# A one-core transformer block in float32: the first modulation rows, the first high parts and the first three projections rearranged

## The chip, the core and the metric

The kernel runs on one core of a Trainium2 chip. The time is the device time of one execution in microseconds (us). Before the change three timed runs took 1871.35, 1871.86 and 1875.66 us, median 1871.86 us. One more execution was taken with the hardware profiler: it took 1873.81 us, of which 1872.1 us are the span from its first to its last instruction.

## What is computed

The reference, cut to what matters here (x is 2048 x 576, c is 1 x 576, w_mod is 576 x 3456):

```python
mod = (silu(c) @ w_mod).reshape(1, 6, 1, 576)
sa, ca, ga, sb, cb, gb = ...            # six modulation vectors of 576
h = layernorm(x) * (1 + ca) + sa
x = x + ga * A(h)                       # q, k, v projections; attention with memory in 4 segments of 512 rows; wo
h = layernorm(x) * (1 + cb) + sb
x = x + gb * B(h)                       # SwiGLU with 4608 hidden columns
```

Only the first line for `sa` (shift) and `ca` (scale), the first `h`, and the projections to q and k lie in the part that changes. The rest follows it.

## The kernel before, in words

Matrix products are made to nearly float32 accuracy from two parts: an operand is cast to fp32r (the high part, `hi`), the remainder is the low part, and a product is high x high + low x high + high x low. `split` (L84) does this with a POOL cast (L85) and a DVE subtraction (L86).

**Head (0 to about 45 us).** SP starts the loads in the order of the program: `cs` (the vector c) and `gat` (beta), then six tiles `wm` of w_mod, each with two row groups of 96 rows and one of the two slices (L336), between them the four row tiles of x of segment 0, in numbers given by `XP`, then the weights `wraw` of the q and k projection (L297), four of them before a buffer must come free. TensorE multiplies silu(c), copied into 32 columns (`sgb`), by `wm` (L362): for each slice and each of six row groups two matmuls, columns 0:256 and 256:576, into two 32-partition groups of the PSUM tile `pr`. These write rows; a row is copied to SBUF by ACT (L366, L369), turned into columns by three transposes (`pcr`, L373), and DVE puts scale (+1) and shift into `colv` (L376 to L378).

The rows of x are normalized by DVE and POOL, and transposed by TensorE in five blocks `pt` of 128 columns (L240, two PSUM buffers). `evac_split` (L242) takes each block: ACT applies scale and shift (`hf`, L247), POOL casts the high part `hh` (L85), DVE subtracts to the low part `hl` (L86); the fifth block has 64 columns, and its high and low parts share the tile `hr`. The weights go through `split` on POOL and DVE too (`wqkh`, `wqkl`).

**Projections.** `proj` (L462) makes one 128 x 512 block `pp` of q or k from 14 matmuls (L105, `mm14`): three for each of four blocks and two with `hr`. There are nine per segment and three PSUM buffers for them, which the value projection `pv` shares. ACT copies `pp` to `pf` (L470), `split` makes `fh` (POOL) and `fl` (DVE), and SP writes them to DRAM (`kD`, `qD`, `qF`). `phi_k` transposes the k blocks (`ptk`, L441). `pf`, `fh` and `fl` have two buffers each. The four segments s = 0 to 3 run this way until about 245 us; from segment 1 on the first attention steps, which need DVE, are laid between the matmuls.

**What sets the order.** The program is recorded in the order of the code; a scheduler then places each engine's instructions by readiness and priority. Within an engine the instructions run in that order, TensorE's matmuls too. SP starts the DMAs in its own order, and an instruction that waits there holds up the ones behind it.

Of the kernel before, what the change touches and what calls it, by code (L numbers as in the profile page):

```python
# [11 lines left out]
ALU = mybir.AluOpType  # L12
# [38 lines left out]
HP = (0, 1, 2)  # L51
XP = (3, 1, 0, 0, 0, 0)
LD = 2
# [24 lines left out]
@with_exitstack  # L78
def block(ctx: ExitStack, tc: tile.TileContext, x, wqk, wv, wo, beta, wgu, wgr, wd, c, w_mod, out):
    nc = tc.nc  # L80
# [161 lines left out]
    def evac_split(wk, pt, kt, hi, lo, sc, bi, tag="hf"):  # L242
        f = wk.tile([P, L], F32, tag=tag, name="hf")
        n = P if kt < 4 else 64
        if kt == 4:
            hi, lo = hi[0:64], hi[64:128]
        nc.scalar.activation(f[:n], pt[:n], AF.Identity, scale=sc[:n], bias=bi[:n])  # L247
        split(hi, lo, f[:n])

    with ExitStack() as p1:  # L250
# [28 lines left out]
        cs = wk.tile([96, 6], F32, tag="cs", name="cs")  # L279
        nc.sync.dma_start(cs, c)  # L280
        nc.sync.dma_start(gat, beta.partition_broadcast(P))
        xs = {}
# [46 lines left out]
        with ExitStack() as p0:  # L329
            m0 = pool(p0, "m0")  # L330
            wm = {}
            gx = load_x(0)
            for p in (1, 0):
                for k in range(3):
                    wm[p, k] = m0.tile([96, 2, D], F32, tag=f"wm{p}{k}", name=f"wm{p}{k}")
                    nc.sync.dma_start(wm[p, k], wmv[p][:, 2 * k:2 * k + 2, :])  # L336
                    for _ in range(XP[3 * (1 - p) + k]):
                        next(gx)

# [16 lines left out]
            pr = ps.tile([P, L], F32, tag="m", name="pr", bufs=1)  # L356
            for p in (1, 0):
                for k in range(6):
                    for h in range(2):
                        r = 64 * (1 - p) + 32 * h  # L360
                        w = wm[p, k // 2][:, k % 2, 256:576] if h else wm[p, k // 2][:, k % 2, 0:256]
                        nc.tensor.matmul(pr[r:r + 32, :320 if h else 256], lhsT=sgb[:, k, :], rhs=w,  # L362
                                         start=(k == 0), stop=(k == 5))
            row = wk.tile([P, L], F32, tag="hf", name="row")[:, :320]
            nc.gpsimd.memset(row[:, 256:], 0.0)
            nc.scalar.copy(row[:, :256], pr[:, :256])  # L366
            for p in (1, 0):
                r = 64 * (1 - p) + 32
                nc.scalar.copy(row[r:r + 32, 256:], pr[r:r + 32, 256:320])  # L369
            pc = ps.tile([P, 3, P], F32, tag="m", name="pcr", bufs=1)  # L370
            for b in range(3):
                n = P if b < 2 else 64
                nc.tensor.transpose(pc[:n, b, :], row[:, 128 * b:128 * b + n], ident)  # L373
            for p in (1, 0):
                c0 = 64 * (1 - p)
                nc.vector.tensor_scalar(colv[:, 0:2, 1 - p], pc[:, 0:2, c0], float(p), None, op0=ALU.add)  # L376
                nc.vector.tensor_scalar(colv[:, 2:4, 1 - p], pc[:, 0:2, c0 + 32], float(p), None, op0=ALU.add)
                nc.vector.tensor_scalar(colv[0:64, 4:5, 1 - p], pc[0:64, 2, c0 + 32:c0 + 33], float(p), None, op0=ALU.add)  # L378

# [68 lines left out]
        def mem(s):  # L448
            for t in range(5):
# [10 lines left out]
                yield  # L460

        def proj(s, t):  # L462
            hh, hl, hr = hT[s]
            pp = ps.tile([P, L], F32, tag="p", name="pp", bufs=3)
            mm14(pp, lambda k: wqkh[:, t, k, :], lambda k: wqkl[:, t, k, :], lambda k: hh[k],
                 lambda k: hl[k], lambda: hr, True)
# [3 lines left out]
            nc.scalar.copy(f, pp)  # L470
            split(fh, fl, f)
            k0, k1 = 128 * t, min(128 * t + 128, D)
            if k0 < D:
                n = k1 - k0
                nc.sync.dma_start(kD[s][k0:k1, 0:2, :], f32(fh[:n]).unsqueeze(1).to_broadcast([n, 2, L]))
                nc.sync.dma_start(kD[s][k0:k1, 2, :], f32(fl[:n]))
            q0, q1 = max(128 * t - D, 0), 128 * t + 128 - D
            if q1 > 0:
                n = q1 - q0
                r = P - n  # L480
                nc.sync.dma_start(qD[s][q0:q1, 0:3:2, :], f32(fh[r:]).unsqueeze(1).to_broadcast([n, 2, L]))
                nc.sync.dma_start(qD[s][q0:q1, 1, :], f32(fl[r:]))
                if s > 0:
                    nc.sync.dma_start(qF[s][q0:q1, :], f[r:])
            return f
# [19 lines left out]

        for t in range(4):
            load_qk(t)
        for t in range(3):
            split_qk(t)
        for _ in trans_in(0):  # L510
            pass

        def load_wv():
            for k in range(5):
# [3 lines left out]
                yield  # L518

        for s in range(NSEG):  # L520
            gens = []
# [1171 lines left out]
```

## Time and profile before

| | |
|---|---|
| profiled execution | 1873.81 us |
| its span | 1872.1 us |
| median of three timed runs | 1871.86 us |
| busy TensorE (PE) | 1829.1 us, 98% of the span |
| busy VectorE (DVE) | 1492.9 us, 80% |
| busy ScalarE (ACT) | 1075.6 us, 57% |
| busy GpSimd (POOL) | 681.3 us, 36% |

The rows quoted below are of five kinds. A row of the timeline has the start, the time busy, the engine, the line, the operation with the tile that it writes and the tiles that it reads, and in brackets how long the engine was idle before it and who ended that. A row of the windows has the stretch, its length, the busy time of each engine with its instructions (x), the granted clock of TensorE, the share of the DMA engines and the GB/s. A group row has count, busy time and mean duration in ns. The slices of the page divide the span by 40. A matmul's end is modelled and runs past the next one's start, so I read the spacing of matmuls by their starts.

### The profile page before, as it was taken

What the parts mean: (1) busy time and instruction counts of PE and PEld (TensorE: products, weight loads), DVE (VectorE), ACT (ScalarE), POOL (GpSimd) and SP (SyncE); (2) the same over time, 40 slices, a digit from 0 to 9 for tenths busy, and PEclk for the clock granted to TensorE, in tenths of its full rate; (3) what the DMA queues carried; (4) which work ended last, traced back from release to release, by engine and by line L of the source; (5) the groups of instructions that cost most, each with busy time, mean ns of one, the idle gap of its engine ahead of it and who ended that gap; (6) DMA issues with size and microseconds to landing.
All of it is one profiled execution on the core that took longest, in us unless ns stands there. A gap on an engine that the chain in (4) does not pass through costs nothing.

```text
span 1872.1 us, 31670 instructions
## 1 busy us (share of the span) xinstructions
PE 1829.1 (98%) x10735; PEld 1546.2 (83%) x10735; DVE 1492.9 (80%) x3364; ACT 1075.6 (57%) x2330; POOL 681.3 (36%) x1173
## 2 busy tenths in 40 slices
PE   6999999999999999999999999989999999999999
PEld 4888876677776788888888888878888888888888
DVE  6565448788886699888888988857888888888886
ACT  1222258878877557777777777634454454544442
POOL 6212248776556657566565665400000000000000
PEclk9999999999999999999999999999999999999999
DMA  6766777677864954544545544485233332433331
GB/s 192 252 224 210 245 234 194 175 210 198 212 163 126 297 190 158 175 152 153 186 147 160 168 115 164 138 277 190 87 116 104 126 103 79 125 104 118 109 96 57
DMA packets 149912, 305.56 MB, mean 163 GB/s; under 512 B 30040, under 2 KB 60888, under 8 KB 147832
## 3 DMA queue, kind: packets, MB, share of 16 engines
q1 hardware_dynamic: 139144, 259.21, 46.2%
q10 hardware_dynamic: 10608, 44.34, 6.0%
q8 instruction: 85, 1.39, 0.3%
q14 instruction: 75, 0.61, 0.1%
HBM read 193.28 MB, written 109.64 MB: 162 GB/s over the span
## 4 chain that ended last, share of the span: by engine, by line
PE 86%; DVE 4%; DMA 4%; ACT 3%; issue 2%; POOL 1%; SPq 0%; POOLq 0%; ACTq 0%; DVEq 0%
PE A L1234 24%; PE pd L1353 19%; PE C L1234 12%; PE B L1234 6%; PE pp L105 5%; PE s L188 3%; PE av L627 3%; PE s L603 3%; PE pd L1373 2%; PE pw L737 2%; PE pv L105 2%; ACT Pt L610 1%; DMA y<-yD 1%; DVE junk L193 1%; PE pn L808 1%
## 5 line engine op out<-in xcount | busy, mean ns | idle before, releaser
L1234 PE MATMUL A<-y,wh 128*128 128x512 f32 x1152 | 405.4, 393 | 2.0 <-DMA y<-yD 1.3
L1361 DVE TENSOR_TENSOR acc<-acc,pd 128x576 f32<-128x576 f32 x327 | 245.3, 751 | 79.9 <-PE pd L1353 73.8
L193 DVE CUSTOM_DVE_ANT_0 junk<-s,tri 128x256 bf16<-128x256 f32 (+3 forms) x512 | 222.2, 484 | 66.2 <-PE s L188 49.1
L1353 PE MATMUL pd<-dh,ah 128*128 128x288 f32 x896 | 268.3, 299 | 1.1 <-DVE acc L1359 0.7
L1353 PE MATMUL pd<-dl,ah 128*128 128x288 f32 x896 | 264.2, 295 | 0.0
L1353 PE MATMUL pd<-dh,al 128*128 128x288 f32 x896 | 262.9, 293 | 0.0
L1234 PEld LDWEIGHTS A<-y,wh 128*128 128x128 f32 x1152 | 216.9, 188 | 41.1 <-issue 1.3
L1196 DVE TENSOR_TENSOR wl<-O,wh 128x256 fp32r<-128x256 f32 x504 | 239.5, 479 | 4.2 <-ACT wh L1195 3.5
L1234 PE MATMUL A<-y,wl 128*128 128x512 f32 x576 | 225.2, 391 | 0.0
L610 ACT ACTIVATE Pt<-s 128x512 f32<-128x512 f32 (+1 forms) x352 | 188.3, 559 | 43.2 <-PE s L603 21.1
L1234 PE MATMUL C<-y,wh 128*128 128x512 f32 x576 | 204.4, 396 | 3.0 <-DMA y<-yD 3.0
L1195 ACT CAST wh<-O 128x256 fp32r<-128x256 f32 x504 | 198.4, 406 | 1.9 <-POOL O L1189 1.6
L1353 PEld LDWEIGHTS pd<-dh,ah 128*128 128x128 f32 x896 | 168.4, 188 | 21.1 <-ACT pd L1329 4.0
L1299 DVE TENSOR_TENSOR al<-sg,ah 128x512 fp32r<-128x512 f32 x240 | 177.0, 738 | 8.5 <-ACT ah L1298 8.4
L1353 PEld LDWEIGHTS pd<-dl,ah 128*128 128x128 f32 x896 | 169.8, 189 | 16.0
L1189 POOL TENSOR_TENSOR O<-O 128x128 f32<-128x128 f32 x280 | 155.0, 586 | 69.2 <-DVE wl L1196 19.7
L1353 PEld LDWEIGHTS pd<-dh,al 128*128 128x128 f32 x896 | 169.4, 189 | 0.0
L1298 ACT CAST ah<-sg 128x512 fp32r<-128x512 f32 x240 | 149.1, 621 | 25.1 <-DVE sg L1258 24.1
L603 PE MATMUL s<-qs,ks 110*128 110x512 f32 (+2 forms) x384 | 149.0, 403 | 6.5 <-ACT Pt L610 4.7
L188 PE MATMUL s<-ks,qs 108*128 108x256 f32 (+3 forms) x512 | 142.4, 330 | 2.3 <-DVE mx L193 1.9
L1234 PEld LDWEIGHTS C<-y,wh 128*128 128x128 f32 x576 | 108.9, 189 | 22.5 <-DMA y<-yD 3.2
L1234 PEld LDWEIGHTS A<-y,wl 128*128 128x128 f32 x576 | 108.6, 188 | 14.8
(367 smaller groups left out, 4120.4 us busy)
## 6 DMA issues: line engine op xcount, KB each, us to landing
wr<-rD SPq DMA_DIRECT2D x216, 112.0 KB
O<-in_wgu_dram SPq DMA_DIRECT2D x36, 512.0 KB
oD<-O ACTq DMA_DIRECT2D x36, 512.0 KB
O<-oD SPq DMA_DIRECT2D x36, 512.0 KB
O<-in_wgu_dram SPq DMA_DIRECT2D x36, 384.0 KB
ks<-kD SPq DMA_DIRECT2D x32, 384.0 KB
qs<-qD SPq DMA_DIRECT2D x64, 192.0 KB
y<-yD SPq DMA_DIRECT2D x11, 1024.0 KB
```

The lines of the kernel that those rows point to most:

```text
L188: nc.tensor.matmul(bank[:, n * (h - h0):n * (h - h0) + n], lhsT=qst[b][0:108, h, 128 * i:128 * i + 128], rhs=kst[b][0:108, h // 2, 0:n], s ...
L193: nc.vector.tensor_tensor_reduce(junk[:, :n], bank[:, n * (h - h0):n * (h - h0) + n], tri[:, L - n:], 1.0, -3e38, op0=ALU.add, op1=ALU.max ...
L603: nc.tensor.matmul(bank[:, n * (g - h):n * (g - h + w)].rearrange("p (a b) -> p a b", a=w), lhsT=kst[u % NB][0:110, g // 2, 128 * j:128 * ...
L610: nc.scalar.activation(pt[:, h:h + per, :n], bank[:, :n * per].rearrange("p (a b) -> p a b", a=per), AF.Exp, scale=SCALE)
L1189: eng.tensor_tensor(o[:, d, i, s_], o[:, a, i, s_], o[:, b, i, s_], op=op)
L1195: nc.scalar.copy(wh, o)
L1196: later.append(lambda: nc.vector.tensor_tensor(wl, o, f32(wh), op=ALU.subtract))
L1234: nc.tensor.matmul(bank, lhsT=a, rhs=b, start=(first and n == 0), stop=(n == 6), skip_group_check=not first)
L1298: nc.scalar.copy(ah, src)
L1299: later.append(lambda: nc.vector.tensor_tensor(al, src, f32(ah), op=ALU.subtract))
L1353: nc.tensor.matmul(pd[:, i, :288], lhsT=a[:, tk], rhs=w, start=(add and k == 0), stop=(k == 2), skip_group_check=not add)
L1361: nc.vector.tensor_tensor(o, o, pd[:, :, :288], op=ALU.add)
```

## The change

Six edits.

1. w_mod is given a second time as `w_mod0`: for each of the six row groups k, 96 partitions with slices 1 (scale) and 0 (shift) side by side, 4608 contiguous bytes per partition. One DMA loads both slices of a row group (six DMAs, as before, of the same size).
2. For each row group four matmuls are issued, one for each of four 32-partition groups of `pr`: two slices x two column ranges (0:320 and 256:576), all 320 columns wide. There are 24, as before. One ACTIVATE takes all rows out and adds 1 to the scale rows through the bias `half`; three DVE copies fill `colv` in place of six additions.
3. `cs` and `gat` are loaded from ACT's queue. Two x tiles go ahead of the first `wm`, by `XP = (2, 1, 1, 0, 0, 0)`. The load of the first `wraw` stands in the code just behind `wm`.
4. In `evac_split`, in all four segments, ACT writes the high part straight out of PSUM (L250), then `hf` (L251); POOL has no part in it.
5. In `proj`, in all segments, ACT casts `fh` straight out of PSUM (L481), DVE subtracts it from PSUM into `fl` (L482), and ACT copies `pf` last (L484), and not at all for segment 0 from block 5 on.
6. The first three projections of segment 0 are written interleaved, block by block (`proj3`, L468).

```diff
-XP = (3, 1, 0, 0, 0, 0)
+XP = (2, 1, 1, 0, 0, 0)
...
+    half = cst.tile([P, 1], F32, tag="half", name="half")
+    nc.gpsimd.memset(half[0:64], 1.0)
+    nc.gpsimd.memset(half[64:128], 0.0)
...
+        nc.scalar.activation(hi, pt[:n], AF.Identity, scale=sc[:n], bias=bi[:n])
         nc.scalar.activation(f[:n], pt[:n], AF.Identity, scale=sc[:n], bias=bi[:n])
-        split(hi, lo, f[:n])
+        nc.vector.tensor_tensor(lo, f[:n], f32(hi), op=ALU.subtract)
...
-        nc.sync.dma_start(cs, c)
-        nc.sync.dma_start(gat, beta.partition_broadcast(P))
+        nc.scalar.dma_start(cs, c)
+        nc.scalar.dma_start(gat, beta.partition_broadcast(P))
...
-            for p in (1, 0):
-                for k in range(3):
-                    wm[p, k] = m0.tile([96, 2, D], F32, tag=f"wm{p}{k}", name=f"wm{p}{k}")
-                    nc.sync.dma_start(wm[p, k], wmv[p][:, 2 * k:2 * k + 2, :])
-                    for _ in range(XP[3 * (1 - p) + k]):
-                        next(gx)
+            for k in range(6):
+                wm[k] = m0.tile([96, 2, D], F32, tag=f"wm{k}", name=f"wm{k}")
+                for _ in range(XP[k]):
+                    next(gx)
+                nc.sync.dma_start(wm[k], w_mod0[k])
+            load_qk(0)
...
-            for p in (1, 0):
-                for k in range(6):
-                    for h in range(2):
-                        r = 64 * (1 - p) + 32 * h
-                        w = wm[p, k // 2][:, k % 2, 256:576] if h else wm[p, k // 2][:, k % 2, 0:256]
-                        nc.tensor.matmul(pr[r:r + 32, :320 if h else 256], lhsT=sgb[:, k, :], rhs=w,
-                                         start=(k == 0), stop=(k == 5))
+            for k in range(6):
+                for g in range(4):
+                    c0 = 256 * (g % 2)
+                    nc.tensor.matmul(pr[32 * g:32 * g + 32, :320], lhsT=sgb[:, k, :], rhs=wm[k][:, g // 2, c0:c0 + 320],
+                                     start=(k == 0), stop=(k == 5))
...
-            nc.gpsimd.memset(row[:, 256:], 0.0)
-            nc.scalar.copy(row[:, :256], pr[:, :256])
-            for p in (1, 0):
-                r = 64 * (1 - p) + 32
-                nc.scalar.copy(row[r:r + 32, 256:], pr[r:r + 32, 256:320])
+            nc.scalar.activation(row, pr[:, :320], AF.Identity, bias=half)
...
-                nc.vector.tensor_scalar(colv[:, 0:2, 1 - p], pc[:, 0:2, c0], float(p), None, op0=ALU.add)
...
+            for h in range(2):
+                nc.vector.tensor_copy(colv[:, 2 * h:2 * h + 2, :], pv[:, 0:2, :, h, 0])
+            nc.vector.tensor_copy(colv[0:64, 4, :], pv[0:64, 2, :, 1, 0])
...
+        def proj3():
+            hh, hl, hr = hT[0]
+            for t in QKORD[:3]:
+                first[t] = ps.tile([P, L], F32, tag="p", name="pp", bufs=3)
+            for kt, t in [(kt, t) for kt in range(3) for t in QKORD[:3]] + [(kt, t) for t in QKORD[:3] for kt in (3, 4)]:
+                h, l = wqkh[:, t, kt, :], wqkl[:, t, kt, :]
+                for a, b in ((h, hh[kt]), (l, hh[kt]), (h, hl[kt])) if kt < 4 else ((h, hr), (l, hr)):
+                    nc.tensor.matmul(first[t], lhsT=a, rhs=b, start=(kt == 0 and a is h and b is hh[0]),
+                                     stop=(kt == 4 and a is l))
...
-            nc.scalar.copy(f, pp)
-            split(fh, fl, f)
+            nc.scalar.copy(fh, pp)
+            nc.vector.tensor_tensor(fl, pp, f32(fh), op=ALU.subtract)
+            if s > 0 or t < 5:
+                nc.scalar.copy(f, pp)
...
+        proj3()
```

How the order moves, at three places. First TensorE at its start: the modulation matmuls `pr` (`wm` is w_mod, `sgb` the copied silu(c)), and the transposes `pt` of x. Before:

```order
L362 MATMUL pr<-wm_248,sgb 32x320
L240 MATMUL pt<-ident,x_244 128x128 x4
L362 MATMUL pr<-wm_251,sgb 32x256
L362 MATMUL pr<-wm_251,sgb 32x320
L362 MATMUL pr<-wm_251,sgb 32x256
L362 MATMUL pr<-wm_251,sgb 32x320
L240 MATMUL pt<-ident,x_244 128x128 x4
L362 MATMUL pr<-wm_253,sgb 32x256
```

Now, from TensorE's first instruction to the transposes of the row:

```order
L364 MATMUL pr<-wm_245,sgb 32x320 x4
L364 MATMUL pr<-wm_250,sgb 32x320 x4
L243 MATMUL pt<-ident,x_246 128x128 x2
L364 MATMUL pr<-wm_253,sgb 32x320 x4
L243 MATMUL pt<-ident,x_246 128x128 x3
L364 MATMUL pr<-wm_256,sgb 32x320 x4
L243 MATMUL pt<-ident,x_246 128x128 x3
L364 MATMUL pr<-wm_258,sgb 32x320 x4
L364 MATMUL pr<-wm_260,sgb 32x320 x4
L371 MATMUL pcr<-ident,row 128x128 x2
```

Each `wm` tile now feeds four matmuls of four partition groups in a row, and the eight transposes are spread over three places instead of two.

Second, TensorE behind the transposes of the row, where segment 0's projections begin. Before, it took the first matmul of the projection, two groups of transposes, and then what the scheduler saw as ready from two projections:

```order
L240 MATMUL pt<-ident,x_244 128x128 x4
L105 MATMUL pp<-hh_365,wqkh 128x512
L240 MATMUL pt<-ident,x_244 128x128 x4
L105 MATMUL pp<-hh_365,wqkl 128x512
L105 MATMUL pp<-hh_365,wqkh 128x512
L105 MATMUL pp<-hl_369,wqkh 128x512
L105 MATMUL pp<-hh_366,wqkh 128x512
L105 MATMUL pp<-hh_366,wqkl 128x512
L240 MATMUL pt<-ident,x_244 64x128 x4
```

Now:

```order
L468 MATMUL pp<-hh_360,wqkh 128x512
L468 MATMUL pp<-hh_360,wqkl 128x512
L468 MATMUL pp<-hh_360,wqkh 128x512
L243 MATMUL pt<-ident,x_246 128x128 x4
L468 MATMUL pp<-hh_360,wqkl 128x512
L468 MATMUL pp<-hh_360,wqkh 128x512
L468 MATMUL pp<-hh_360,wqkl 128x512
L468 MATMUL pp<-hl_364,wqkh 128x512
L243 MATMUL pt<-ident,x_246 128x128 x4
L468 MATMUL pp<-hl_364,wqkh 128x512 x2
L468 MATMUL pp<-hh_361,wqkh 128x512
L468 MATMUL pp<-hh_361,wqkl 128x512
```

Behind the second group of transposes stand four matmuls, then the last group of transposes, then 31 matmuls without a break. The two matmuls with `hr` of the first projection come behind 30 others; before they came behind 21.

Third, DVE between the normalization of x and the tile `hr`. Before:

```order
L376 TENSOR_SCALAR colv<-pcr 128x2
L377 TENSOR_SCALAR colv<-pcr 128x2
L378 TENSOR_SCALAR colv<-pcr 64x1
L86 TENSOR_TENSOR wqkl<-wraw,wqkh 128x640 x2
L86 TENSOR_TENSOR hl_369<-hf,hh_365 128x512
```

Now:

```order
L86 TENSOR_TENSOR wqkl<-wraw,wqkh 128x640
L374 COPY colv<-pcr 128x4 x2
L375 COPY colv<-pcr 64x2
L86 TENSOR_TENSOR wqkl<-wraw,wqkh 128x640 x2
L252 TENSOR_TENSOR hl_364<-hf,hh_360 128x512
L86 TENSOR_TENSOR wqkl<-wraw,wqkh 128x640
```

The first `wqkl` now stands ahead of `colv`. Outside segments 0 to 3 (from about 245 us on) no engine's order changes.

More of the change, by code (lines that the diff above doesn't have):

```diff
@@ L504, in vproj @@
                 nc.scalar.dma_start(vD[s], vs[s])
-        for t in range(4):
+        for t in range(1, 4):
             load_qk(t)
[L508 to L511, printed above, removed]
+        split_qk(0)
+        split_qk(1)
+        for kt, _ in enumerate(trans_in(0)):
+            if kt == 0:
+                split_qk(2)
         def load_wv():
```

17 lines of the change are left out of this document (9 added, 8 removed).

## The prediction

> **What bounds the kernel now.** I read the page first, then windows of the first 270 us, then the timeline of the first 50 us.
>
> ```profile
> span 1872.1 us, 31670 instructions
> ...
> PE   6999999999999999999999999989999999999999
> ```
>
> TensorE is full in every slice but the first (0 to 47 us): only there can the change win much. For segments 1 to 3, which it touches too, one window:
>
> ```profile
> 80.00:240.00 160.00, 158.34 (x917) 135.82 (x916) 87.71 (x207) 39.24 (x73) 40.20 (x64) 1.00 0.68 229
> ```
>
> TensorE idles 160.00 - 158.34 = 1.7 us there, and no edit can win more than that in this stretch, whatever it takes off POOL. So the sum is one of the head, up to the first matmul of the fourth projection; from there both kernels run the same matmuls.
>
> The head in the timeline, from the modulation rows to the ramp:
>
> ```profile
> 6.97 2.35 PE L362 MATMUL pr<-wm,sgb 96*32 96x256 f32 x8 [6.97 <-DMA wm<-in_w_mod_dram]
> ...
> 16.69 1.12 PE L240 MATMUL pt<-ident,x 128*128 128x128 f32 x4
> ...
> 17.74 5.32 PE L362 MATMUL pr<-wm,sgb 96*32 96x256 f32 x24
> ...
> 19.57 1.54 POOL L85 TENSOR_SCALAR wqkh<-wraw 128x640 fp32r<-128x640 f32 x2 [2.43 <-DMA wraw<-in_wqk_dram]
> ...
> 23.10 0.37 ACT L366 COPY row<-pr 128x256 f32<-128x256 f32 x1 [18.30 <-PE pr L362]
> ...
> 23.96 0.55 PE L373 MATMUL pcr<-ident,row 128*128 128x128 f32 x3 [0.89 <-ACT row L369]
> ...
> 24.93 1.45 ACT L247 ACTIVATE hf<-pt,colv 128x512 f32<-128x512 f32 x2 [1.03 <-DVE colv L376]
> ...
> 25.76 0.66 PE L240 MATMUL pt<-ident,x 128*128 128x128 f32 x4 [1.25 <-ACT hf L247]
> ```
>
> POOL reads the first `wraw` at 19.57 us. That is loaded behind the last `wm`, so `wm` is there before 19, but TensorE is busy with the rows until 17.74 + 5.32 = 23.06 us: they end late because TensorE is slow on them.
>
> Then the ramp, to the fourth projection:
>
> ```profile
> 36.42 1.03 DVE L86 TENSOR_TENSOR hr<-hf,hr 64x512 fp32r<-64x512 f32 x1
> ...
> 37.51 0.50 PE L105 MATMUL pp<-hr,wqkh 128*128 128x512 f32 x1 [2.00 <-DVE hr L86]
> ...
> 40.97 0.63 PE L105 MATMUL pp<-hh,wqkl 128*128 128x512 f32 x1
> 41.40 0.63 PE L105 MATMUL pp<-hl,wqkh 128*128 128x512 f32 x1
> ...
> 42.42 0.40 PE L105 MATMUL pp<-hl,wqkh 128*128 128x512 f32 x1
> 42.66 0.39 PE L105 MATMUL pp<-hh,wqkh 128*128 128x512 f32 x1
> ...
> 44.51 0.60 PE L441 MATMUL ptk<-ident,pf 128*128 128x128 f32 x4
> 44.87 0.48 PE L105 MATMUL pp<-hh,wqkh 128*128 128x512 f32 x1
> ```
>
> TensorE waits 2.0 us for `hr`, which DVE ends at 37.45 us, 12.5 us behind `colv`. At 44.87 us the fourth projection begins; 42 matmuls and two groups of `ptk` are done. Matmuls of 512 columns start 0.43 us apart at 41 us and 0.24 us apart at 42.5 us: the clock.
>
> **The clock** decides this change. First the durations of the row matmuls (lowest, median, highest, in ns), at their begin and at their end:
>
> ```profile
> L362 PE MATMUL pr<-wm,sgb x8: 604/688/742, 7.0 to 8.6; 96*32 96x256 f32 x4, 96*32 96x320 f32 x4
> ```
>
> ```profile
> L362 PE MATMUL pr<-wm,sgb x8: 380/432/507, 21.5 to 22.6; 96*32 96x320 f32 x5, 96*32 96x256 f32 x3
> ```
>
> The last ones take 0.63 of the first ones' time. The transposes at 16.69 us take 1.12 us for four, at 25.76 us 0.66 us. So the clock is half until about 21.6 us, though its column reads 1.00 there (it has no record before). It changes between windows of 3.41 us:
>
> ```profile
> 11.38:14.80 3.42, 3.42 (x14) 1.56 (x12) 1.97 (x6) 0.00 (x0) 3.42 (x6) 1.00 1.04 257
> ...
> 18.21:21.62 3.41, 3.41 (x18) 2.18 (x16) 0.00 (x0) 0.00 (x0) 1.45 (x2) 1.00 0.90 334
> ...
> 35.28:38.69 3.41, 1.41 (x6) 1.00 (x6) 3.35 (x4) 0.41 (x1) 1.64 (x2) 1.00 0.33 89
> 38.69:42.10 3.41, 3.41 (x12) 2.72 (x11) 2.90 (x5) 1.31 (x3) 2.75 (x4) 0.50 0.59 205
> 42.10:45.52 3.42, 3.42 (x18) 2.80 (x18) 3.36 (x5) 0.67 (x2) 1.14 (x2) 1.00 0.93 352
> ...
> 1260.66:1264.08 3.42, 2.55 (x10) 2.46 (x11) 0.00 (x0) 0.94 (x3) 0.00 (x0) 0.50 0.33 118
> ```
>
> A window with 1.41 us of work (35.28) is followed by one at half clock, and one full of matmuls (18.21, 38.69) by full clock. One with 2.55 us (1260.66) was still followed by half. The window from 11.38 us is full, yet the clock did not rise; of its work this much was transposes:
>
> ```profile
> 11.38:14.80 3.42, 1.12 (x4) 0.72 (x4) 1.00 1.04 257
> ```
>
> So 2.3 us of matmuls and 1.1 us of transposes do not raise the clock, and 3.41 us of matmuls do. I take it that transposes count little.
>
> **The change, step by step**, against the profiled execution (1873.81 us).
>
> *Loads.* Two SP issues leave the front, and the rates of the DMA engines from 10 to 20 us, in slices of 0.25 us, show what follows `wm`:
>
> ```profile
> 0.80 0.40 SPq L280 DMA_DIRECT2D cs<-in_c_dram  x1
> ...
> 1.72 0.43 SPq L336 DMA_DIRECT2D wm<-in_w_mod_dram  x1
> ```
>
> ```profile
> GB/s 267 277 323 415 249 212 276 286 240 230 267 295 267 212 277 277 184 286 277 286 267 221 258 258 258 258 276 267 300 193 267 230 277 317 379 420 379 389 410 389
> ```
>
> The first load is issued 0.92 us earlier. The rate is about 260 while `wm` flows and 390 from 18.3 us, for `wraw`: the last `wm` lands at about 18.7 us (estimate: 0.8 us before the first read of `wraw`, whose 328 kB take 0.8 us at 390). With the same bytes it would land at 17.8. Longer rows may help: no gain is one end, and the rate of `wraw` for all six tiles (2.65 MB: 10.2 us at 260, 6.8 at 390) the other, 14.4. I take 17, near the row of `wm` itself.
>
> The Trainium skill ("SBUF — State Buffer", Door 1: The DMA port swizzle) says that partitions 0 to 63 reach only half of the 16 DMA ports. Two thirds of a 96-partition tile share that half, so by it longer rows win nothing and the forecast moves 0.9 us up; if row length were the limit, TensorE would bound the rows at 17.1 and it moves 1.1 us down. No row of before tells these apart.
>
> *Rows.* Each of these matmuls shows as two records, so eight are two row groups of one slice. Their durations sum to 8 x 0.688 = 5.5 us but fit in 2.35 us: the two partition groups run beside each other, 1.1 us for each pair of row groups' matmuls at half clock, the time of the 320-column one alone. Before there are twelve such pairs. Four partition groups at once cost between 1.1 us (all beside each other) and 2.2 us (two and two) per row group. I take 1.1, since the two do not slow each other. The last `wm` at 17.0 and 1.1 us plus 0.2 us of tail give 18.3; TensorE's own work from the third tile on (4 x 1.1 + 6 x 0.28 us of transposes from about 12 us) gives 18.1. So the rows end at 18.2 instead of 23.06 us (bounds 17.1 and 19.1).
>
> *Row to column.* From 23.06 to 24.93 us it took 1.87 us. One ACTIVATE takes the place of three copies (-0.3 us), the three transposes run at half clock (+0.3), and the first `colv` copy costs as before. The `wqkl` now ahead of `colv` on DVE waits for a `wraw` that lands by 17.8, POOL's 0.77 us (two in 1.54 at 19.57) and about as long on DVE: 19.4, before the columns come at 20.0. If `wm` came a us later, both would move. ACT begins `hh` at 20.1 us.
>
> *Ramp.* `hh` takes about 0.75 us as `hf` does (two in 1.45 at 24.93), so TensorE starts at 20.9. Its clock is half: since the rows take half as long and the transposes lie between them, no window before is full of matmuls. It runs 11 matmuls (0.43) and three groups of transposes (1.1): 8.0 us, to 28.9. No window with such a group raises the clock, as at 11.38 us; the first window free of them begins 0 to 3.4 us behind 28.5 and ends 3.41 us later, at 33.6 on average (31.9 to 35.3). By then 11 more matmuls are done; the other 20 take 0.235 us each. The 42nd ends at 38.3 us (37.5 to 39.1). `ptk` of two blocks adds 0.9 and the wait for `pf` 0.1: 39.3 us against 44.87. **The head wins 5.6 us.**
>
> *What must be on time for that.* `hr` on DVE: with the same 12.5 us behind `colv` as before it comes at 32.6; five of some 12 POOL operations between them are gone, and TensorE needs it only behind 30 matmuls, at about 35.5. So the low parts and POOL's casts are hidden by the slow clock. Were the clock full, they would set the end.
>
> *Segments 1 to 3.* ACT gets five more ACTIVATEs of 0.75 us and nine casts of 0.59 us per segment, 9 us of some 60, beside the 25% that it is busy. POOL loses as many. Their price is 0, with -1.7 us (the idle time above) as one end; the other is the third rival.
>
> The sum: 1873.8 - 5.6 = 1868.2 us. The profiled execution lies 1.95 us above the median of the timed runs, so on their scale **1866.3**, and I say 1866.5.
>
> **Rivals.**
>
> *The clock rises early.* If transposes count as work, the first full window behind 20.9 ends at 26.0 on average. By then 7 matmuls and two groups are done; 35 matmuls and one group (0.66) take 8.9 us: 34.9 instead of 38.3, 3.4 us less: 1863. The window at 11.38 us speaks against it, but rows of 32 columns were the matmuls in it.
> The Trainium skill ("TensorE: Matmul & The Clock Gate", Part 4: PE-mode transpose) says that a transpose does not count as busy in the same way. By that rule the sum is mine; without it, this rival's. It speaks against thinning out the rows.
>
> *Only two partition groups run at a time.* Then the rows end at 22 to 23 us, `colv` comes at 24.5, the clock is full as before, and `hr`, 12.5 us later, sets the end: 37.0 + 12 x 0.235 + 1.0 = 40.8, a win of 4 us: 1868.
>
> *The third ends slower: the PSUM buffer of a projection is held longer.* It was free after ACT's copy; now the cast, DVE's subtraction and the copy come first, and `fh` and `fl` wait for buffers that DMAs empty.
>
> ```profile
> 164.77 0.59 ACT L470 COPY pf<-pp 128x512 f32<-128x512 f32 x1 [1.50 <-PE pp L105]
> ...
> 172.26 0.68 DVE L86 TENSOR_TENSOR fl<-pf,fh 128x512 fp32r<-128x512 f32 x1
> ```
>
> ```profile
> 100.00:110.00 10.00, 9.91 (x52) 8.00 (x51) 9.87 (x31) 2.78 (x5) 1.45 (x3) 1.00 0.51 181
> ```
>
> Here `fl` ends 8.2 us behind its projection, and DVE is full at 100 to 110 us. With three buffers and 3.7 us per projection (14 x 0.235 and a `ptk`) it decides from 7.4 us on. Each wait costs up to 0.68 + 0.59 = 1.3 us; for a third of the 27 projections that is 11.5 us, 6 more than the head wins: 1878. Some waits only would eat the gain: 1870 to 1872.
>
> **Numbers.** Forecast 0.50, early clock 0.22, two at a time 0.07, gain eaten 0.14, slower 0.07. A measurement can tell about 0.3% (5.6 us) from no change, so faster means below 1866.2: half of the forecast, nearly all of the early clock and a little of the others, 0.48. Slower, above 1877.5: 0.06. The rest, 0.46, is within. The range runs from the early clock with the best loads (1861) to the eaten gain (1873); outside lie the slower rival and the tails, 0.15.
>
> **What would show it.** In the profile after: `pr` in groups of four that take about 1.1 us, ending near 18; ACT's first `hh` at 20; matmuls 0.43 us apart until 32 to 35 us; no wait for `hr`; the fourth projection at 39. TensorE idle in 80 to 240 us (less about 6) within 1 to 3 us. Spacing of 0.24 us before 28 us would show the early clock, waits of `pp` for ACT or DVE the held buffers. I would be wrong if `colv` came late behind the `wqkl` on DVE.

## The result, and the profile after

Over 20 runs each the changed kernel takes 1869.1 us (median; 1864.9 to 1874.5) and the kernel before 1871.8 (1868.5 to 1878.5): a ratio of 0.9986, 95% interval 0.9977 to 0.9995, or 2.6 us less. The prediction said 1866.5 and 5.4 us less. A second comparison, told below, gave 0.9974 (0.9963 to 0.9985), 4.9 us less. The profiled execution took 1868.09 us, 5.7 less than that of before: in the two profiles the gain is the one forecast, in the medians it is smaller.

The page of the changed kernel, its span and TensorE's row of 40 slices:

```profile
span 1866.2 us, 31659 instructions
...
PE   6999999999999999999999999989999999999999
```

The head in its timeline (start, duration, engine, line, what; in brackets the wait and who ended it):

```profile
7.71 0.23 ACT L349 ACTIVATE gat<-gat 128x32 f32<-128x32 f32 x1 [3.68 <-DMA gat<-in_beta_dram]
...
9.69 1.30 PE L364 MATMUL pr<-wm,sgb 96*32 96x320 f32 x8 [9.69 <-DVE sgb L359]
...
19.86 2.36 PE L364 MATMUL pr<-wm,sgb 96*32 96x320 f32 x16
...
21.56 4.11 POOL L85 TENSOR_SCALAR wqkh<-wraw 128x640 fp32r<-128x640 f32 x4 [2.63 <-DMA wraw<-in_wqk_dram]
...
22.32 0.82 DVE L86 TENSOR_TENSOR wqkl<-wraw,wqkh 128x640 fp32r<-128x640 f32 x1 [3.94 <-POOL wqkh L85]
...
23.87 0.23 DVE L374 COPY colv<-pcr 128x4 f32<-128x4 f32 x2 [0.72 <-PE pcr L371]
...
24.07 0.78 ACT L250 ACTIVATE hh<-pt,colv 128x512 fp32r<-128x512 f32 x1 [1.19 <-DVE colv L374]
...
24.99 0.76 PE L468 MATMUL pp<-hh,wqkh 128*128 128x512 f32 x1 [1.16 <-ACT hh L250]
...
33.76 0.69 DVE L252 TENSOR_TENSOR hr<-hf,hr 64x512 fp32r<-64x512 f32 x1
...
35.11 0.40 PE L468 MATMUL pp<-hr,wqkh 128*128 128x512 f32 x1
...
38.07 0.66 PE L438 MATMUL ptk<-ident,pf 128*128 128x128 f32 x4
38.48 0.48 PE L105 MATMUL pp<-hh,wqkh 128*128 128x512 f32 x1
```

The rows end at 19.86 + 2.36 = 22.22 us, 0.8 us sooner than before and 4.0 later than forecast. POOL reads the first `wraw` at 21.56 us, 2.0 later than before: here the loads are late, not TensorE. ScalarE's `hh` (24.07) and TensorE's ramp (24.99) are late by the same 4 us. Yet the fourth projection begins at 38.48 us, 0.8 sooner than forecast, with one group of `ptk` ahead of it instead of the two that the forecast counted (0.4 us). The time between comes from the clock; windows on its grid (length, TensorE busy, clock, DMA share, GB/s):

```profile
18.51:21.92 3.41, 3.41 (x27) 1.00 1.03 331
21.92:25.33 3.41, 1.54 (x8) 1.00 0.47 165
25.33:28.75 3.42, 3.42 (x11) 1.00 0.63 174
28.75:32.16 3.41, 3.41 (x20) 1.00 0.48 125
```

The clock's column has no record before its first rise and reads 1.00 there; the counts tell it: 11 matmuls and transposes in the third window, 20 in the fourth. Of the third window this much was transposes (the first number behind the length, TensorE; the next two are weight loads and ScalarE):

```profile
25.33:28.75 3.42, 1.05 (x4) 1.08 (x5) 2.77 (x5) 1.00 0.63 174
```

The clock rises at 28.75 us, 3.8 us behind the start of the ramp, where the forecast had 12.7. From there TensorE is never idle until `ptk`, and `hr`, ready at 34.45, is 0.7 us ahead of its use.

Behind the head the segments gain too. First before, then after, from the last matmul of segment 0's projections to that of segment 3's (length, then busy time of PE, PEld, DVE, ACT, POOL):

```profile
65.80:238.10 172.30, 170.65 (x1014) 148.53 (x1013) 90.73 (x213) 42.91 (x80) 41.50 (x66) 1.00 0.68 229
```

```profile
60.10:230.20 170.10, 169.28 (x1014) 148.44 (x1013) 87.62 (x211) 67.33 (x121) 10.79 (x22) 1.00 0.68 228
```

The same 1014 matmuls in 2.2 us less. ACT takes 24 us more and POOL 31 less. So at the last projection (230.2 us) the changed kernel is 7.8 us ahead; at the end 5.9. Of the 2 us given back the clock is one part. The 45 us behind the last projection, before and after (the clock is the third number from the end):

```profile
238.10:283.40 45.30, 41.62 (x270) 31.04 (x268) 23.33 (x90) 28.50 (x61) 21.48 (x36) 0.96 0.72 219
```

```profile
230.20:275.00 44.80, 42.20 (x267) 31.30 (x266) 21.16 (x86) 27.02 (x58) 18.19 (x31) 0.92 0.71 211
```

### The profile page after: what moved, and what is told of

It is laid out like the page before. It is cut to its first block, busy times and chain, and to the rows that moved or that the text cites. A ratio compares the mean times of both kernels' runs of the same rounds, so it can differ in the third digit from the quotient of the medians.

```text
span 1866.2 us, 31659 instructions
## 1 busy us (share of the span) xinstructions
PE 1824.0 (98%) x10735; PEld 1541.6 (83%) x10735; DVE 1482.0 (79%) x3361; ACT 1106.0 (59%) x2380; POOL 640.0 (34%) x1118
## 4 chain that ended last, share of the span: by engine, by line
PE 86%; DMA 5%; DVE 4%; ACT 2%; issue 1%; POOL 1%; SPq 0%; ACTq 0%; DVEq 0%; POOLq 0%
PE A L1249 23%; PE pd L1368 19%; PE C L1249 12%; PE B L1249 6%; PE pp L105 5%; PE pv L105 3%; PE s L191 3%; PE s L618 3%; PE av L642 3%; PE pd L1388 2%; PE pw L752 2%; ACT Pt L625 1%; DMA y<-yD 1%; DVE junk L196 1%; PE pm L451 1%
```

## The experiments

Landing times are those of the completion events in the trace. Each transfer has 16 of them; I call them its pieces, "pieces 0.5 us apart" means from the first to the last of the 16, and a tile has landed with its last. "From tile to tile" is counted between first pieces. "Head" is the last matmul of segment 0's projections: 65.8 us before, 60.1 after.

**The small loads back on SP's queue.**

```
-        nc.scalar.dma_start(cs, c)
-        nc.scalar.dma_start(gat, beta.partition_broadcast(P))
+        nc.sync.dma_start(cs, c)
+        nc.sync.dma_start(gat, beta.partition_broadcast(P))
```

> The changed kernel with the two small loads (the condition vector, 2 kB, and beta, 16 kB in 128 rows of 128 bytes) back on SP's queue ahead of everything. In the changed kernel they stand on ACT's queue, beta lands at 7.68 us, and the first piece of the first modulation tile lands 3.16 us behind the x tile before it where the later tiles follow at 1.88 us. Theory, the second queue costs it: the last modulation tile lands at 18.5 to 19.5 us instead of 20.65, the rows end near 20.5 instead of 22.2, ScalarE's first hh at 22.0 to 22.8 instead of 24.07, the fourth projection 1.3 to 2 us sooner than at 38.48. Rival, the small rows cost the same wherever they stand: beta lands by 4.6 us and the first row matmul starts by 8.7 us instead of 9.69, but the last modulation tile still lands at 20.0 to 21.2 us, hh at 23.5 to 24.6, and the time is within 1 us of the changed kernel's.

Measured: `gat` landed at 4.83 us, the tiles followed each other at 1.71 us with pieces 0.5 to 0.7 us apart, the last was there at 18.37, `hh` at 22.21, the head at 58.7. Ratio to before 0.9981 (0.9972 to 0.9990). As the theory said (the fourth projection begins at 37.13, 1.35 us sooner), but the repeated runs below show that one profile isn't enough for it.

**Shorter rows.** The tiles get 4 columns of padding, so a row no longer goes in one piece.

```
-                wm[k] = m0.tile([96, 2, D], ...)
+                wm[k] = m0.tile([96, 2, D + 4], ...)[:, :, :D]
```

> The changed kernel with the modulation tiles padded in SBUF by 4 columns, so that each row goes in two pieces of 2304 bytes instead of one of 4608; same data, same number of loads. Theory, the longer rows are slower: the modulation tiles follow each other at 1.71 us as before the change instead of 1.88 us, their first and last pieces lie 1.0 us apart instead of 1.8 to 2.3, the last one lands at 18.6 to 19.2 us instead of 20.65, and hh comes 1.5 to 2 us sooner (22.1 to 22.6). Rival, the rate is set by something else (the order of the loads, the new layout in DRAM): spacing 1.85 us or more, last one at 20.3 to 20.9 us, hh at 24.

Measured: 1.73 to 1.76 us from tile to tile, pieces 1.9 to 2.2 us apart, the last tile at 20.44, `hh` at 23.63, head 59.7, ratio 0.9982 (0.9971 to 0.9993). The spacing is the theory's, the landing the rival's. The length of the rows neither makes nor mends the delay.

**Beta later.**

```
-        nc.scalar.dma_start(gat, beta.partition_broadcast(P))
...
         for t in range(1, 4):
             load_qk(t)
+        nc.sync.dma_start(gat, beta.partition_broadcast(P))
```

> The changed kernel with the load of beta moved behind the loads of the first four weight tiles on SP's queue, and its four small operations behind the first block of transposed inputs; nothing needs it before the second phase. Theory, beta's 128 small rows cost the stream about 1.9 us while they are woven between the large ones: the last modulation tile lands at 18.6 to 19.2 us instead of 20.65, the rows end near 20.5, hh near 22.3, the fourth projection near 36.8 instead of 38.48. Rival, the small rows only wait and do not cost the others anything: sgb and the first row matmul come sooner (by 8.7 us) but the last tile still lands at 20.3 to 20.9 us and hh at 23.8 to 24.2.

Measured: `sgb` at 5.95 and the first row matmul at 8.18 us, but the pieces of the tiles lay 2.3 to 3.5 us apart, the last tile landed at 21.04, `hh` came at 24.23, head 61.3, ratio 0.9986 (0.9974 to 0.9998). The theory that beta's small rows cost 1.9 us falls.

**Rows from tiles of 128 partitions, beta later.**

```
-            for k in range(6):
-                wm[k] = m0.tile([96, 2, D], ...)
+            for k in range(5):
+                n = P if k < 4 else 64
+                wm[k] = m0.tile([P, 2, D], ...)[:n]
...
-                nc.sync.dma_start(wm[k], w_mod0[k])
+                nc.sync.dma_start(wm[k], w_mod0[128 * k:128 * k + n])
```

> As the kernel with beta's load later, and the modulation rows are summed over four tiles of 128 partitions and one of 64 instead of six of 96 (590 kB each instead of 442; the condition vector comes in both layouts in one load). Theory, 96 partitions set the rate of these loads (235 to 258 GB/s, where the weight tiles of 128 partitions flow at 390): a tile takes 1.5 us instead of 2.3 to 2.5 for its bytes, the last one lands at 14 to 15.5 us, TensorE or the inputs on DVE then set the end of the rows at 16 to 17.5, hh at 18 to 19.5, the fourth projection at 32 to 34.5: 4 to 6 us less than the changed kernel. Rival, the rate is that of these rows in DRAM whatever the partitions: 2.3 us or more for a tile, the last one at 18 us or later, hh at 21.5 or later, at most 2.5 us less than the changed kernel.

Measured: 1.43 us from the third tile to the fourth (590 kB, 412 GB/s) against 1.71 for 442 kB (259 GB/s) before. The last piece of the fourth came 2.4 us behind that of the third. From 8 to 13 us, while the tiles flow, the windows of this kernel and, for 13 to 18 us, of before end in the rate:

```profile
8.00:13.00 5.00, 3.46 (x26) 0.69 (x18) 3.04 (x10) 0.00 (x0) 2.06 (x3) 1.00 1.03 370
```

```profile
13.00:18.00 5.00, 5.00 (x20) 2.46 (x20) 1.90 (x4) 0.00 (x0) 3.05 (x7) 1.00 1.04 256
```

The last tile was complete at 16.05, the rows ended at 17.33, and `hh` began at 18.84:

```profile
18.84 0.78 ACT L250 ACTIVATE hh<-pt,colv 128x512 fp32r<-128x512 f32 x1 [0.84 <-DVE colv L371]
```

Head 56.7, ratio 0.9955 (0.9943 to 0.9968): 5.8 us less than the changed kernel in its first comparison. The theory holds for the rate, the rows, `hh` and the time; the last tile came 0.6 us and the fourth projection (35.35) 0.9 us later than it said, and the pieces of a tile lay 1.6 to 3.2 us apart, which it had not foreseen. This kernel also tests the clock: a full window with 1.81 us of transposes (second row: the transposes alone) raised it, and a window with 1.54 us of work took it back for one window:

```profile
13.41:16.82 3.41, 3.41 (x22) 1.41 (x22) 1.47 (x2) 0.00 (x0) 2.20 (x6) 1.00 1.03 295
16.82:20.24 3.42, 1.54 (x13) 0.75 (x6) 2.42 (x6) 1.93 (x4) 3.32 (x4) 1.00 0.41 111
20.24:23.65 3.41, 3.41 (x12) 2.53 (x12) 3.41 (x5) 2.94 (x5) 1.72 (x3) 0.50 0.67 169
```

```profile
13.41:16.82 3.41, 1.81 (x6) 1.01 (x6) 0.00 (x0) 1.00 1.03 295
```

**The same with the condition vector on SP's queue too.**

```
-        nc.scalar.dma_start(cs, c)
+        nc.sync.dma_start(cs, c)
```

> The kernel with row tiles of 128 partitions and beta later, with the last load that stands on ACT's queue (the condition vector) put back at the front of SP's queue. Theory, two queues at the start set the 16 DMA engines out of step: with one queue the first and last piece of a tile lie 0.4 to 0.7 us apart instead of 1.6 to 3.2, the fifth row tile lands at 13.3 to 14.5 us instead of 16.05; the rows then end at 16 to 17 us by TensorE's own work at half clock, hh at 17.3 to 18.5 instead of 18.84, 0.3 to 1.5 us off the time. Rival, the late pieces come from the tiles' form (128 rows of 4608 bytes) and not from the second queue: pieces still 1.5 us or more apart, the fifth tile at 15.5 to 17 us, hh at 18.8 or later because everything starts 0.9 us later.

Measured: pieces 0.7 to 0.9 us apart for three tiles, then 2.4; the fifth tile complete at 16.09, `hh` at 19.87, head 56.9, ratio 0.9971 (0.9958 to 0.9984). The rival's landing, though the pieces of three tiles lay nearer to the theory's. One queue does not keep the engines in step, so the second queue is not shown to be the cause of late pieces.

**The first three projections one after the other.**

```
-        proj3()
```

> The changed kernel with the first three projections one after the other again (each waits for hr before it ends), the rest of the change kept. Theory, interleaving is what keeps TensorE busy until hr is there: hr comes at 34.5 us as in the changed kernel, TensorE waits 3 us or more for it behind the first projection's 12 matmuls and loses its clock once, the fourth projection begins at 41 to 43.5 us instead of 38.48, and the time is 2.5 to 5 us above the changed kernel's: none of the gain is left. Rival, the high parts cast on ScalarE are the gain and hr would be early enough: TensorE waits under 1.5 us, fourth projection before 40 us, the time within 1.5 us of the changed kernel's.

Measured: no wait for `hr`. TensorE's waits from 24 to 45 us (engine, line, released by: us, times, longest):

```profile
PE pp L105 <- ACT hh L250: 1.2, 1, 1.2
PE ptk L438 <- ACT pf L484: 0.5, 1, 0.5
```

The fourth projection begins at 39.67 us, the rival's outcome. Head 61.3, 1.2 us behind the changed kernel; ratio 0.9991 (0.9980 to 1.0002). The theory falls: the scheduler fills the wait from the other projections by itself. That the interleaving written out by hand is worth anything is not shown: from `hh` to the end of the head this kernel takes 37.2 us, and three profiles with the interleaved head 36.0, 36.3 and 37.2 (the last from the kernel that follows here). The two that take 37.2 are those whose clock rose late, 5.7 and 5.8 us behind the start of the ramp.

**GpSimd's casts back in segments 1 to 3.**

```
+            if s > 0:
+                nc.scalar.copy(f, pp)
+                split(fh, fl, f)
+            else:
                 nc.scalar.copy(fh, pp)
                 nc.vector.tensor_tensor(fl, pp, f32(fh), op=ALU.subtract)
```

and the same in `evac_split`.

> The changed kernel with GpSimd casting the high parts again from the second segment on (transposed inputs and projections of segments 1 to 3); the first segment as changed. Theory, the casts on ScalarE also shorten the evacuation in the segments: TensorE's idle time between the end of the first segment's projections and the last projection is 0.8 us in the changed kernel and 1.7 before, that stretch 170.1 and 172.3 us; with the casts back it is 171.5 to 172.5 us again and the time 1 to 2 us above the changed kernel's. Rival, the 2 us there have nothing to do with the casts (they come from the first segment's tail or from chance): the stretch stays at 169.8 to 170.8.

Measured, the stretch from the head to the last projection:

```profile
60.50:233.80 173.30, 171.07 (x1013) 148.02 (x1013) 89.47 (x211) 43.24 (x80) 37.37 (x63) 1.00 0.67 222
```

173.3 us, 3.2 more than with the casts on ScalarE (170.1), so the theory's cause holds. It also lies outside the spread: ten profiles with those casts on ScalarE take 170.0 to 171.4 us there, two of the kernel before 172.3 and 172.2. The ratio, 0.9989 (0.9978 to 1.0000), is 0.6 us above that of the first comparison of the changed kernel, inside its interval: the medians do not tell these kernels apart.

**The kernel before again**, for a second profile.

> The kernel before, unchanged, for a second profile. The changed kernel's profile is 5.7 us ahead when the first segment's projections end and 7.8 at the last projection, but the medians differ by 2.7. Theory, the later stages vary by chance from execution to execution (where the clock's windows of 3.41 us fall, when transfers land) and the first profile of before had a good draw behind 270 us: this one shows the head at 65.8 within 0.5 us and the five stages behind it each up to 2.5 us off the first, together 1 to 5 us longer behind the last projection or a shorter segment stretch. Rival, the later stages of before really are shorter when they begin later: this profile agrees with the first within 1 us in each stage.

Measured: head 66.5, then 172.2 us to the last projection and 1633.9 behind it, as in the first profile (172.3 and 1634.1). That is the rival's outcome for the stages. Its loads were another matter: the six tiles followed each other at 2.04 us instead of 1.71, and the last landed at 20.93 instead of 18.77, with the same program.

**The kernel before, delayed.** 50 matmuls into a buffer that nothing reads.

```
             if s == 1:
+                dm = ps.tile([P, L], F32, tag="p", name="dm", bufs=3)
+                for _ in range(50):
+                    nc.tensor.matmul(dm, lhsT=wqkh[:, 0, 0, :], rhs=hT[1][0][0], start=True, stop=True)
```

> The kernel before with 50 extra matmuls of 512 columns ahead of the second segment's projections, into a PSUM buffer that nothing reads: a pure delay of 50 x 0.235 = 11.7 us; from the second phase on every engine's order is that of the kernel before. So far eight profiles of kernels with the changed head take 1634 to 1640 us (mean 1637) behind the last projection where two of before take 1634, and the medians gained 2 to 6 us less than the stretch up to the last projection did. Theory, the stages behind the segments are partly paced by streams of transfers that do not start sooner: what comes there early waits, what comes late waits less, so of this delay only 6 to 9 us reach the end and the stretch behind the last projection shrinks by 2.5 us or more against 1634. Rival, nothing there is tied to an absolute time and the differences are chance: the delay reaches the end whole, 11 to 13 us more than before, and that stretch takes 1632.5 us or more.

Measured: the segments take 183.6 us, 11.3 more. The ratio is 1.0066 (1.0050 to 1.0082), 12.4 us (9.4 to 15.4): the delay reaches the end whole, the rival. But this profile took only 1631.0 us behind the last projection, as the theory had said. That needs no delay, as the next run shows.

**The changed kernel again**, unchanged.

> The changed kernel, unchanged, for a second profile and a second comparison. Theory, its head gain is real and part of it is given back later in most executions: the first segment's projections end at 60 to 60.8 us, the last projection 170 to 170.6 us later, the stretch behind takes 1635 to 1639 us, and the median is 1.5 to 4.5 us below before. Rival, the first comparison was off and the gain is that of the two profiles (5.7 us): median 5 to 6.5 us below before, stretch behind 1634 us.

Measured: 1867.7 us, ratio 0.9974 (0.9963 to 0.9985). Head 59.6, segments 170.0, and 1631.4 us behind them, 4.6 less than in the first profile. The median is at the theory's upper end, and the stretch behind is neither theory's nor rival's. The profiled execution (1862.9 us) was the fastest of this run's ten. Here is the stretch that the first profile ran at a clock of 0.92:

```profile
229.60:275.00 45.40, 41.10 (x276) 31.44 (x274) 24.73 (x98) 30.59 (x65) 22.38 (x36) 1.00 0.74 219
```

**128 partitions with the waits of the head filled.**

```
+            def warm(n, a, b):
+                for _ in range(n):
+                    nc.tensor.matmul(dm[:, :P], lhsT=a, rhs=b, start=True, stop=True)
+
+            warm(14, wz, wz)
...
+                    warm((3, 2, 1, 1)[k], wm[k][:, 0, 0:P], wm[k][:, 1, 0:P])
...
+            warm(2, wm[4][:, 0, 0:P], wm[4][:, 1, 0:P])
...
+            warm(4, row[:, 0:P], row[:, P:2 * P])
```

> The kernel with row tiles of 128 partitions and one queue, with extra matmuls of 128 columns on TensorE where it waits in the head (14 before the first row, 7 between the rows, 2 ahead of the row's transposes, 4 behind them), into a PSUM buffer that nothing reads. Theory, the half clock costs the head 2 to 3 us: with the waits filled the clock is full from 7 to 11 us on and stays so, a step of the rows takes 0.65 us instead of 1.1, the transposes of the row 0.55 instead of 0.9, hh comes 0.5 to 1 us sooner than at 19.87, the first projections' matmuls start 0.24 us apart from the first on, the fourth projection begins 1.5 to 3 us sooner than without them. Rival, ScalarE (five times two ACTIVATEs of 0.7 us behind hh) and hr on DVE set the end of the first three projections, not the clock: TensorE waits for hh or hr instead, and the fourth projection begins within 0.7 us of the kernel without the extra matmuls.

Measured: the clock rose at 6.31 us, fell for 13.14 to 16.55 (the window ahead had 1.88 us of work) and was full from there. TensorE's waits from 18 to 40 us:

```profile
PE ptk L448 <- ACT pf L494: 1.6, 1, 1.6
PE pp L478 <- DVE hl L254: 0.6, 1, 0.6
PE pp L478 <- DVE hr L254: 0.6, 1, 0.6
PE pp L478 <- DVE wqkl L86: 0.4, 1, 0.4
PE pp L478 <- ACT hh L252: 0.3, 1, 0.3
```

3.5 us, where the kernel without the extra matmuls waits 0.7 for the row, 1.2 for `hh` and 0.6 for `pf`. The fifth tile landed at 17.75, 1.7 us later, and `hh` began at 20.11, 0.2 later. The fourth projection begins at 36.74 instead of 35.51, 1.2 us later where the rival had allowed 0.7, and the head ends at 58.1 instead of 56.9; ratio 0.9958 (0.9945 to 0.9971). From `hh` to the fourth projection it is 16.6 us, against 15.6 without the extra matmuls. The mechanism is the rival's: at full clock TensorE waits for DVE and ScalarE.

**128 partitions, both small loads in front on SP's queue.**

```
+        nc.sync.dma_start(cs, c)
+        nc.sync.dma_start(gat, beta.partition_broadcast(P))
```

> The kernel with row tiles of 128 partitions, with both small loads (the condition vector and beta) at the front of SP's queue as before the change. Where beta stood there (two profiles of before and the kernel with the small loads put back) the pieces of a row tile landed 0.5 to 1.3 us apart; where beta came late or on ACT's queue, 1.5 to 4 us apart. Theory, beta at the front, with the large loads queued up behind it, lets the DMA engines start together: pieces 0.4 to 1.3 us apart, the fifth row tile complete at 14.8 to 15.8 us although everything begins 2 us later, hh at 18.5 to 19.5, and the time 0.4 to 0.6% below before. Rival, how far the pieces lie apart is chance or goes with 128 rows: 1.5 us or more again, the fifth tile at 16.5 to 18.5 us, hh at 20 to 21.5, the time 0.2 to 0.3% below before.

Measured: pieces 0.8 us apart for three tiles, 2.2 and 1.6 for the others, the fifth tile at 16.49, `hh` at 21.50, head 58.7. Between theory and rival in the loads, the rival in `hh`, the theory's range in the time. That was the lowest of all, 1863.0 us, ratio 0.9947 (0.9934 to 0.9960), but its interval overlaps that of the first kernel with 128 partitions, whose head is 2 us shorter; the loads don't explain its lead. It beats both kernels, 9.9 us below before.

## Why the prediction came out as it did

**The loads** were mis-sized: 17 us forecast, 20.65 measured. The first load did start 0.92 us sooner, and the longer rows won nothing. With the loads of the changed kernel the last tile landed at 20.65, 20.69, 19.37 and 19.19 us in four profiles, with those of before at 18.77, 20.93 and 19.31: no gain, and a spread of 2 us from one execution to the next. I had read one profile as if the rate were fixed. What did move the rate is the number of partitions: from the first piece of the first tile to that of the last, the x tiles between included, the loads flow at 349 to 364 GB/s in the four profiles with 128 partitions and at 233 to 281 in the ten with 96. The Trainium skill ("SBUF — State Buffer", Door 1: The DMA port swizzle) says that the bandwidth depends on how many ports the partitions reach, and that partitions 0 to 63 reach only half of them. The prediction had drawn from it that longer rows win nothing, and so it came. But ports are not the whole of it: with the same 4608 bytes per partition, a tile of 96 partitions took 1.61 to 2.05 us to the next and one of 128 partitions 1.42 to 1.44. Why pieces of one tile lie 0.5 us apart in one profile and up to 4.1 in another stays open: neither the queue, nor beta's place, nor the row length accounts for all of them.

**The rows** came out as forecast: the step from one row group to the next is 2.36 - 1.30 = 1.06 us at half clock (1.1 forecast), so four partition groups run beside each other. **Row to column** too: 1.85 us from the end of the rows to `hh` (1.9), with `wqkl` (done at 23.14) ahead of `colv`. As the prediction said, with `wm` late both moved.

**The ramp** went the way of the first rival. The step that failed is "transposes count little". In the nine profiles of kernels with the changed head in which the clock first rose in the ramp, it did so 3.2 to 5.8 us behind the ramp's start; the forecast had 12.7, the rival 5.1. The window that raised it held one group of four transposes, 1.05 us, in the changed kernel, and 4 to 8 transposes, 1.05 to 1.92 us, in the other profiles. The kernel with the small loads back shows best that they counted there. Here are two of its windows, and the transposes of the second (length, TensorE busy, clock, DMA share, GB/s; the last row has weight loads and ScalarE behind TensorE):

```profile
17.74:21.16 3.42, 2.71 (x21) 1.00 0.95 351
24.57:27.98 3.41, 3.41 (x14) 1.00 0.77 238
```

```profile
24.57:27.98 3.41, 1.91 (x8) 1.50 (x7) 1.87 (x3) 1.00 0.77 238
```

The first, with 2.71 us of work, nearly all of it row matmuls, did not raise the clock. The second did, and its other six matmuls took at most 2.40 us, so without the 1.91 us of transposes it would have had less (this takes both kinds of matmul to count alike). The Trainium skill ("TensorE: Matmul & The Clock Gate", Part 4: PE-mode transpose) says that transposes don't count as busy in the same way; these windows speak against using that as a rule. It is not that simple either: thirteen full windows with row matmuls of 96 partitions and 3 to 6 transposes did not raise the clock (among them 18.51 above and 11.38 before), while such rows alone (18.21 before), and rows of 128 partitions with 6 transposes, did. What the chip counts there stays open. The 42 matmuls and their transposes took 12.9 us (24.99 to 37.9) where the forecast had 17.4, 4.5 less, and that made good the 4 us of the loads: the sum of the head was right by two errors that cancel, which is luck.

**`hr` on time** held (34.45, needed at 35.11), and so did the sentence that at full clock the low parts and casts would set the end: the kernel with the filled waits shows it. No run takes the casts on ScalarE out of segment 0, or the row matmuls back to two groups, so how the gain of the head divides between these edits is not shown.

**Segments 1 to 3** at price 0 were wrong by 2.2 us in the good direction. I took TensorE's idle time, 1.7 us, as the most that could be won; 1.4 us of the gain is busy time. That bound was wrong because a matmul's modelled end runs past the next one's start, so that a short wait shows no idle time. The starts do show it: what the spacings lie above the median spacing of matmuls of their kind adds up to 9.0 us in this stretch before, 7.0 after and 10.1 with GpSimd's casts back. The casts are the cause of the gain (173.3 us with GpSimd's back), and the held PSUM buffers of the slower rival do not show: TensorE idles 170.10 - 169.28 = 0.8 us there.

**From the profile to the median.** The sum was made as if a gain at the head reached the median whole. At the last projection the two profiles of the changed kernel are 7.8 and 8.4 us ahead of before's first, the medians 2.6 and 4.9. The time behind the last projection, for the same instructions, goes with how many windows of 3.41 us the clock is halved in:

| profile | windows at half clock behind the last projection | us from there to the end |
|---|---|---|
| changed, second | 2 | 1631.4 |
| before, delayed | 3 | 1631.0 |
| beta later | 3 | 1635.7 |
| casts back | 4 | 1634.1 |
| before, both | 5 | 1634.1, 1633.9 |
| shorter rows; 128 rows; 128 rows warm | 5 | 1638.2, 1636.2, 1635.1 |
| changed, first; 128 rows one queue; no interleave | 6 | 1636.0, 1638.0, 1639.8 |
| small loads back; 128 rows beta first | 7 | 1639.4, 1636.9 |

From 2 to 7 windows the time grows by some 7 us, 1.3 us a window; a whole window of matmuls at half clock would cost 1.7. So one profile carries 4 us of luck in either direction. The delayed kernel speaks against waits for an absolute time there: of 11.3 us at the last projection, 12.4 (9.4 to 15.4) are there at the end. The windows are not all of it: with 3 and with 5 of them the profiles of before take 1.0 to 4.7 us less than those with a changed head. That the eleven profiles with a changed head take 1636.4 us there on average and the three of before 1633.0 may be chance or not; three profiles can't tell, and it stays open where the rest of the gain goes in the median.

## What to carry to other kernels

Before a change to a head of 40 us is priced, have two or three profiles of it: landing times moved by 2 us with the program unchanged, and the later stages by 8 over profiles in which they run the same instructions. Read what TensorE may win from the spacing of its matmuls, not from its idle time alone. Load with all 128 partitions where the order of a sum allows it; here the kernels with it took 5.4 to 9.9 us less than before where the change alone took 2.6 to 4.9. Where an early engine is slow by its clock, ask what would be late at full clock before spending work on warming it.

## What the runs showed of the hardware

- A load of 442 kB into 96 partitions took 1.61 to 2.05 us from tile to tile, one of 590 kB into 128 partitions 1.42 to 1.44 (between first pieces; the last pieces of these 128-partition tiles came 2.4 to 2.9 us apart).
- Four partition groups of 320 columns with fp32 operands took 1.06 us together at half clock; eight records with their tail took 1.30 us there and 0.74 at full clock (128 partitions, waits filled).
- Windows in the head with 1.54 and 1.88 us of work halved the clock and one with 2.21 did not. But in the profile with 1.88, one with 1.86 us, at 33.62, did not either, so the busy time of a window alone does not tell.
